# Zero products ahead of the first chunk, a later read of the shared accumulators, and a second gate buffer on one Trainium2 core

## The chip, the cores and the metric

The kernel runs on one core of a Trainium2 chip. The metric is the device time of one launch in microseconds (us), lower is better. All inputs and outputs are float32. The names of the engines are those of the profile: PE is the matrix engine (TensorE; PEld is its weight load), DVE is VectorE, ACT is ScalarE, POOL is GpSimd, and SP (SyncE) issues nearly all of the DMAs.

## What is computed

Three layers in a row: an attention with a pooled and a local part, a bilinear layer, and a layer that multiplies by its own softmax and normalises. The reference, cut to what matters:

```python
B, H, S, D = 4, 8, 576, 64           # attention
q_d, k_d, v_d = (t.reshape(B, H, S // 4, 4, D).mean(axis=3) for t in (q, k, v))
out_d = softmax(scale * q_d @ k_d.T) @ v_d              # 144 pooled positions
mask = np.abs(pos[:, None] - pos[None, :]) < 4
out_local = softmax(np.where(mask, scale * q @ k.T, -1e9)) @ v
x = np.repeat(out_d, 4, axis=2) + out_local             # to 2304 tokens x 512
x = (x @ w_a) * (x @ w_b) @ w_out                       # 512 -> 1536 -> 512
h = x @ w_in                                            # 512 -> 1024
solu = h * softmax(h)
ln = (solu - mean(solu)) / sqrt(var(solu) + 1e-6) * g_ln
out = ln @ w_out2                                       # 1024 -> 512
```

## The kernel before

The 2304 tokens are cut into five blocks: four of 512 tokens (`WIDE`) and a last one of 256. The bilinear layer goes through the 1536 hidden columns in 12 chunks of 128. A chunk of a block is two groups of 12 products into two PSUM tiles called `ab` (`emit_A`, one for `w_a` and one for `w_b`), then a copy of the first to the gate buffer `a` by ACT (`emit_a`), a multiplication by the second on DVE (`emit_mult`), a split of the result into a high part `ph` (ACT) and a low part `pl` (POOL) in `emit_p`, and 12 products into four accumulators (`emit_B`). Every matrix product of these layers is made of three, high by high, high by low and low by high, so the weights are split as well (`w_stages`: `raw` is loaded, then two passes on ACT, two on DVE that write `wm`, a cast on ACT and a subtraction give `w`).

The four accumulators of a wide block are two PSUM tiles `acc0` and `acc1` and the two halves of one tile that spans two banks, `accS`. At the last chunk of a block each is copied out as `o` as soon as its three products are written, and stored to `o1d` in HBM. In the last block two tiles of 512 columns hold all four, each half a tile, and the two `ab` halves of a chunk also share a tile.

Ahead of the first chunk stands the attention of the first 512 tokens. Its pooled part per pair of heads `hp` is: sums of `qkr` to `qkds` (DVE), scores `S` (PE), a maximum `pm` (DVE), exponentials `E` (ACT), a division (POOL), transposes `PT` (PE), a copy `PTs` (ACT), and the product `pv` (PE). Its local part for 128 tokens `s` is: scores `lS` (PE), mask, maximum and subtraction to `lP` (DVE), exponential (ACT), sums `lsm` (DVE), a division (POOL), transposes `lPT` (PE), copies `lPTs` (ACT), the product `lo` (PE), the sum with the pooled part `lx` (DVE), and the split into `xTh` (ACT) and `xTl` (POOL or DVE), which are the operands of the first chunk. `A(0, ...)` of the first chunk is cut in columns 0 to 256, which need `s` = 0 and 1, and 256 to 512, which need 2 and 3.

The order of the work is a list of due times written out by hand (`first` and `add`), played by `advance`. In block 0 the order on every engine is pinned to that list (`pin`), in blocks 1 to 3 that of PE alone, and the rest and the whole last block are ordered by the scheduler's own simulation. An engine takes its instructions strictly in that order.

The third layer (`emit_C` writes `h`, `emit_D` writes `o` from the transposed `cT`) starts in the waits of the last block and then fills the last 170 us.

## Time and profile before

| | |
|---|---|
| runs | 800.87, 805.21, 806.71 us; median 805.21 |
| profiled execution | 803.08 us, of which the span from first to last instruction is 801.3 |
| busy in the span | PE 765.4 us (96%), DVE 376.9 (47%), ACT 332.5 (41%), POOL 228.5 (29%) |
| mean granted TensorE clock | 0.988 of full speed |
| DMA | 85.04 MB, 106 GB/s over the span |

A row of a timeline gives the start, the time that the row covers, the engine, the line of the kernel, the operation with its tiles and shape, and how many instructions were merged. In square brackets stands how long the engine sat idle before and what ended that. [...] A plain float32 product shows as two rows for each instruction, a transpose and the rounded products (`ab`, `acc`, `h`, `o`) as one.

### The profile page before, as it was taken

How to read it: one execution, taken by the hardware profiler on the slowest of the kernel's cores; microseconds unless marked ns; L12 is line 12 of the kernel's file. 1: busy time of each engine (PE TensorE's matmuls, PEld its weight loads, DVE VectorE, ACT ScalarE, POOL GpSimd, SP SyncE). 2: the span in 40 equal slices, each digit the busy share in tenths (PEclk: the TensorE clock that was granted, in tenths of full speed). 3: DMA queues.
4: the chain of work that ended last, by engine and by line, in shares of the span. 5: the costliest groups of instructions: out<-in, count | busy, mean ns of one | idle time of the engine just before them, and what ended most of it. 6: DMA issues, size and time to landing. Idle time of an engine off the chain costs nothing.

```text
span 801.3 us, 12378 instructions
## 1 busy us (share of the span) xinstructions
PE 765.4 (96%) x4848; PEld 621.3 (78%) x4848; DVE 376.9 (47%) x689; ACT 332.5 (41%) x691; POOL 228.5 (29%) x204
## 2 busy tenths in 40 slices
PE   4979999998999999999999999999899999999997
PEld 3867777776787787777787888888788888888885
DVE  5678889974223324223213220126765373545441
ACT  3648777653222324322323221147645343344432
POOL 1242343431322222232111121114222352334320
PEclk9979999999999999999999999999999999999999
DMA  8977844214212203111102000036422554444321
GB/s 239 239 259 246 268 152 137 70 30 139 59 57 61 83 30 110 59 52 34 42 15 80 15 27 1 0 112 208 155 79 66 157 173 144 145 134 145 103 79 40
DMA packets 65226, 85.04 MB, mean 106 GB/s; under 512 B 9016, under 2 KB 46136, under 8 KB 65168
## 3 DMA queue, kind: packets, MB, share of 16 engines
q1 hardware_dynamic: 64864, 84.02, 33.8%
q8 instruction: 38, 0.62, 0.3%
q10 hardware_dynamic: 304, 0.23, 0.1%
q14 instruction: 20, 0.16, 0.1%
HBM read 66.93 MB, written 17.30 MB: 105 GB/s over the span
## 4 chain that ended last, share of the span: by engine, by line
PE 81%; DVE 7%; ACT 5%; DMA 3%; issue 3%; POOL 1%; SPq 0%; DVEq 0%; ACTq 0%; POOLq 0%
PE ab L473 33%; PE o L616 13%; PE h L548 11%; PE acc L507 8%; PE accS L507 7%; PE lo L412 2%; PE pv L283 2%; PE lPT L393 2%; DVE wm L117 2%; DMA qkr<-qkp 1%; PE lS L353 1%; PE S L223 1%; DMA raw<-w 1%; PE PT L266 1%; ACT o L514 1%
## 5 line engine op out<-in xcount | busy, mean ns | idle before, releaser
L473 PE MATMUL ab<-xTh,w 128*128 128x512 f32 (+1 forms) x976 | 298.0, 375 | 6.2 <-DVE a L483 3.6
L473 PEld LDWEIGHTS ab<-xTh,w 128*128 128x128 f32 x976 | 179.9, 191 | 43.7 <-DVE a L483 5.6
L473 PE MATMUL ab<-xTl,w 128*128 128x512 f32 (+1 forms) x488 | 180.2, 369 | 0.9 <-DVE xTl L167 0.5
L490 POOL TENSOR_TENSOR pl<-a,ph 128x512 fp32r<-128x512 f32 (+1 forms) x60 | 75.1, 1251 | 234.6 <-ACT ph L489 234.6
L483 DVE TENSOR_TENSOR a<-a,ab 128x512 f32<-128x512 f32 (+1 forms) x60 | 38.0, 632 | 181.3 <-PE ab L473 181.3
L473 PEld LDWEIGHTS ab<-xTl,w 128*128 128x128 f32 x488 | 93.4, 191 | 15.1 <-DVE xTl L167 0.9
L548 PE MATMUL h<-w,o1w 128*128 128x512 f32 x432 | 103.9, 391 | 1.1 <-ACT w L123 0.9
L548 PEld LDWEIGHTS h<-w,o1w 128*128 128x128 f32 x432 | 80.1, 188 | 18.1 <-ACT w L123 1.1
L616 PE MATMUL o<-w,cTh 128*128 128x512 f32 x288 | 91.0, 397 | 1.2 <-ACT cTh L606 0.9
L507 PE MATMUL acc<-ph,w 128*128 128x512 f32 (+1 forms) x288 | 90.2, 365 | 0.0
L478 ACT COPY a<-ab 128x512 f32<-128x512 f32 (+1 forms) x60 | 32.5, 542 | 108.9 <-PE ab L473 103.7
L507 PE MATMUL accS<-ph,w 128*128 128x512 f32 x192 | 68.0, 391 | 4.2 <-ACT o L514 4.2
L616 PEld LDWEIGHTS o<-w,cTh 128*128 128x128 f32 x288 | 54.0, 188 | 14.3 <-ACT cTh L606 1.1
L489 ACT CAST ph<-a 128x512 fp32r<-128x512 f32 (+1 forms) x60 | 34.6, 577 | 67.2 <-DVE a L483 67.2
L507 PEld LDWEIGHTS acc<-ph,w 128*128 128x128 f32 x288 | 52.2, 189 | 9.1 <-issue 1.2
L616 PE MATMUL o<-w,cTl 128*128 128x512 f32 x144 | 57.2, 397 | 0.1
L507 PE MATMUL acc<-pl,w 128*128 128x512 f32 (+1 forms) x144 | 51.1, 358 | 0.1
L600 POOL TENSOR_TENSOR cTl<-raw,cTh 128x1024 fp32r<-128x1024 f32 x15 | 36.0, 2401 | 44.2 <-ACT cTh L599 36.6
L507 PEld LDWEIGHTS accS<-ph,w 128*128 128x128 f32 x192 | 36.0, 188 | 13.1 <-ACT o L514 5.5
L117 DVE CUSTOM_DVE_ANT_0 wm<-raw,wm 128x1024 uint16<-128x1024 uint16 x52 | 43.4, 845 | 2.3
L255 POOL TENSOR_TENSOR E<-E,ss 72x576 f32<-72x576 f32 x16 | 19.3, 1206 | 81.1 <-DVE ss L253 53.4
L557 DVE TENSOR_REDUCE mx<-h 128x1 f32<-128x1024 f32 x18 | 22.0, 1223 | 43.1 <-PE h L548 43.1
(91 smaller groups left out, 1005.5 us busy)
## 6 DMA issues: line engine op xcount, KB each, us to landing
raw<-w SPq DMA_DIRECT2D x52, 512.0 KB
qkr<-qkp SPq DMA_DIRECT2D x32, 288.0 KB
vd<-v SPq DMA_DIRECT2D x15, 512.0 KB
raw<-vd SPq DMA_DIRECT2D x60, 128.0 KB
vw<-vwin SPq DMA_DIRECT2D x36, 140.0 KB
vp<-vp SPq DMA_DIRECT2D x16, 288.0 KB
o1r<-o1d SPq DMA_DIRECT2D x18, 256.0 KB
out<-ob SPq DMA_DIRECT2D x18, 256.0 KB
```

The costliest lines, as they stand in the source:

```text
L117: DVE.tensor_tensor(out=st["w"], in0=st["w"], in1=st["low"], op=ALU.add)
L255: POOL.tensor_tensor(out=ev, in0=ev, in1=st["ss"].to_broadcast([72, 4, SD]), op=ALU.mult)
L473: PE.matmul(out=abs_[blk, j][n][:, c0:c1], lhsT=w[:, ws], rhs=x[:, k, c0:c1], start=(k == 0 and i == 0), stop=(k == 3 and i == 2), skip_gr ...
L478: ACT.copy(out=a, in_=abs_[blk, j][0])
L483: DVE.tensor_tensor(out=a, in0=a, in1=pb, op=ALU.mult)
L489: ACT.copy(out=ph, in_=a)
L490: POOL.tensor_tensor(out=pl, in0=a, in1=f32(ph), op=ALU.subtract)
L507: PE.matmul(out=accs[blk][m], lhsT=wt[:, ms], rhs=x, start=(j == 0 and i == 0 and (w == WIDE or m % 2 == 0)), stop=(j == NCH - 1 and i == ...
L548: PE.matmul(out=h[:, n * 512:n * 512 + 512], lhsT=x[:, ks], rhs=w, start=(k == 0 and q_ == 0), stop=(k == 3 and q_ == 2))
L557: DVE.tensor_reduce(out=mx, in_=st["h"], axis=AX.X, op=ALU.max)
L600: POOL.tensor_tensor(out=h4(lo), in0=raw, in1=f32(h4(hi)), op=ALU.subtract)
L616: PE.matmul(out=o, lhsT=x[:, k, :], rhs=w, start=(k == 0 and q_ == 0), stop=(k == 7 and q_ == 2))
```

## The change

Three things change. First, products of a tile of zeros, `zz`, are put on PE at ten named places ahead of and in the first chunk: 12 before the first local scores, 9 before those of the second pair of heads, 6 before the fourth, 5 before the first transposes, 7 before the scores `S` of the fourth pair, 6 before the first `lPT`, 10 before the `lo` of `s` = 1, 6 before the second half of `lPT` of `s` = 2, 7 before the columns 256 to 512 of the first chunk, and 4 before the `lS` of `s` = 4. They write to a tile that the following work overwrites, or to one of their own, `fz`. Second, in a wide block the two halves of `accS` are copied out by DVE after the last product of the block, where ACT copied each after its own three products. Third, the gate buffer of the last block is a tile of its own with two buffers, where it was the single buffer of 512 columns.

```diff
+FILL = dict(lS0_0=12, lS0_1=9, lS0_3=6, PT0=5, S3=7, lPT0_0=6, lo1_0=10, lPT2_1=6, A0_256=7, lS4_0=4)
...
+    zz = base.tile([128, 128], F32, name="zz")
+    fz = []
+    def fill(key, out):
+        for _ in range(FILL.get(key, 0)):
+            if out is None:
+                if not fz:
+                    fz.append(ps.tile([128, 512], F32, tag="acc1", name="fz"))
+                out = fz[0][:, 0:128]
+            PE.matmul(out=out, lhsT=zz[:, 0:out.shape[0]], rhs=zz, start=True, stop=True, skip_group_check=True)
...
+            if not b:
+                fill(f"S{hp}", st["S"][0][:, 0:128])
...
+            if not b:
+                fill(f"PT{hp}", st["PT"][0][:, 0:128])
...
+            fill(f"lS{s}_{hps[0]}", None if s > 3 else st["S"][1][:, 384:512])
...
+                fill(f"lPT{s}_{half}", None if s > 1 else pt_[:, 0, :])
...
+                fill(f"lo{s}_{half}", None)
...
+        if (blk, j) == (0, 0):
+            fill(f"A{n}_{c0}", None)
...
     def emit_a(blk, j):
-        a = base.tile([128, WIDE], F32, tag="a", name="a")[:, 0:width[blk]]
+        if width[blk] == WIDE:
+            a = base.tile([128, WIDE], F32, tag="a", name="a")
+        else:
+            a = base.tile([128, 256], F32, tag="a2", bufs=2, name="a")
...
+        def store(m):
+            SP.dma_start(out=o1d[blk][:, :, 128 * m:128 * m + 128].rearrange("i p t -> p i t"),
+                         in_=o1s[blk][:, m, 0:w].rearrange("p (i t) -> p i t", t=128))
...
-                o1 = o1s[blk][:, m, 0:w]
-                ACT.copy(out=o1, in_=accs[blk][m])
-                SP.dma_start(out=o1d[blk][:, :, 128 * m:128 * m + 128].rearrange("i p t -> p i t"),
-                              in_=o1.rearrange("p (i t) -> p i t", t=128))
+                if m < 2 or w < WIDE:
+                    ACT.copy(out=o1s[blk][:, m, 0:w], in_=accs[blk][m])
+                    store(m)
+        if j == NCH - 1 and w == WIDE:
+            for m in (2, 3):
+                DVE.tensor_copy(out=o1s[blk][:, m, 0:w], in_=accs[blk][m])
+                store(m)
...
+    POOL.memset(zz, 0.0)
```

On PE the program began before like this (an entry is a line of the kernel, an operation, its output and inputs, the output's shape and a count of instructions):

```order
L353 MATMUL lS<-qkr 64x70 x4
L223 MATMUL S<-qkds 72x144 x4
L353 MATMUL lS<-qkr 64x70 x4
L223 MATMUL S<-qkds 72x144 x4
L353 MATMUL lS<-qkr 64x70 x8
L223 MATMUL S<-qkds 72x144 x4
L266 MATMUL PT<-id_sb,E 72x72 x8
L223 MATMUL S<-qkds 72x144 x4
L283 MATMUL pv<-PTs,vp 64x144 x16
```

After the change the same stretch on PE reads:

```order
L153 MATMUL lS<-zz 128x128 x12
L372 MATMUL lS<-qkr 64x70 x4
L239 MATMUL S<-qkds 72x144 x4
L153 MATMUL lS<-zz 128x128 x9
L372 MATMUL lS<-qkr 64x70 x4
L239 MATMUL S<-qkds 72x144 x4
L372 MATMUL lS<-qkr 64x70 x4
L153 MATMUL lS<-zz 128x128 x6
L372 MATMUL lS<-qkr 64x70 x4
L239 MATMUL S<-qkds 72x144 x4
L153 MATMUL PT<-zz 72x128 x5
L284 MATMUL PT<-id_sb,E 72x72 x8
```

The real work keeps its order, and the zeros stand between. Further on, PE's order from the transposes of the fourth pair of heads to the `lo` of `s` = 1 is now this, where the entry of `fz` is the only new one:

```order
L284 MATMUL PT<-id_sb,E 72x72 x8
L433 MATMUL lo<-lPTs,vw 64x64 x8
L413 MATMUL lPT<-id_sb,lP 70x128 x8
L433 MATMUL lo<-lPTs,vw 64x64 x8
L301 MATMUL pv<-PTs,vp 64x144 x16
L153 MATMUL fz<-zz 128x128 x10
L433 MATMUL lo<-lPTs,vw 64x64 x16
```

No zeros stand ahead of or behind the transposes `PT` there. On ACT and DVE the order of block 0's start is unchanged.

At the end of block 0 ACT's order was before:

```order
L514 COPY o_2079<-acc_885 128x512
L489 CAST ph<-a 128x512
L514 COPY o_2079<-acc_886 128x512
L514 COPY o_2079<-accS 128x512 x2
L374 ACTIVATE lP<-lP 128x560
```

At the same place DVE's order is after the change:

```order
L509 TENSOR_TENSOR a<-a,ab 128x512
L269 RECIPROCAL ss<-ss 72x4
L549 COPY o_2154<-accS 128x512 x2
L383 TENSOR_TENSOR lP<-lS,mk_sb 128x280 x2
L389 TENSOR_REDUCE lmx<-lP 128x8
```

So two copies have left ACT's queue and stand in DVE's, behind the multiplication of a gate and ahead of a mask.

In the last block PE's order was before, around the first entry of its accumulators (`w_825`, `w_636` and `w_694` are weights of chunks 2, 1 and 0):

```order
L473 MATMUL ab<-xTh,w_825 128x256
L507 MATMUL acc_4938<-ph,w_694 128x256
L507 MATMUL acc_4939<-ph,w_694 128x256
L507 MATMUL acc_4938<-pl,w_694 128x256
L507 MATMUL acc_4938<-ph,w_694 128x256 x2
L507 MATMUL acc_4938<-pl,w_694 128x256
L507 MATMUL acc_4938<-ph,w_694 128x256
L507 MATMUL acc_4939<-pl,w_694 128x256
L507 MATMUL acc_4939<-ph,w_694 128x256 x2
L507 MATMUL acc_4939<-pl,w_694 128x256
L507 MATMUL acc_4939<-ph,w_694 128x256
L473 MATMUL ab<-xTh,w_636 128x256
```

After the change it reads there (`w_900`, `w_1006` and `w_758` are weights of chunks 2, 3 and 0):

```order
L496 MATMUL ab<-xTh,w_900 128x256
L537 MATMUL acc_5013<-ph,w_758 128x256
L537 MATMUL acc_5014<-ph,w_758 128x256
L496 MATMUL ab<-xTh,w_1006 128x256
L496 MATMUL ab<-xTl,w_1006 128x256
L496 MATMUL ab<-xTh,w_1006 128x256 x2
```

The gate products of chunk 3 now begin before the accumulator products of chunk 0 have ended. The rest of the last block is ordered anew on all engines as well. The last 585 instructions of PE are the same in the same order.

## Rows read from the trace of the kernel before

**Rows 1.** The page's first part: busy us, share, instructions.

```profile
PE 765.4 (96%) x4848; PEld 621.3 (78%) x4848; DVE 376.9 (47%) x689; ACT 332.5 (41%) x691; POOL 228.5 (29%) x204
```

**Rows 2.** The waits of PE: total us, times, longest us.

```profile
PE lS L353 <- DMA qkr<-qkp: 9.0, 3, 5.3
PE accS L507 <- ACT o L514: 4.2, 3, 2.5
PE ab L473 <- DVE a L483: 3.6, 3, 2.2
...
PE lo L412 <- DVE lx L424: 2.6, 1, 2.6
```

**Rows 3.** Stretches: busy us of each engine, granted clock, DMA share, GB/s.

```profile
0.00:20.00 20.00, 8.58 (x77) 6.02 (x79) 11.27 (x29) 7.09 (x31) 2.49 (x6) 1.00 0.88 239
...
44.00:45.00 1.00, 1.00 (x19) 0.88 (x18) 0.74 (x1) 0.65 (x2) 1.00 (x1) 0.50 0.98 397
...
193.00:194.00 1.00, 1.00 (x3) 0.73 (x3) 0.93 (x3) 0.00 (x0) 0.00 (x0) 0.50 1.13 335
```

**Rows 4.** Timeline of PE, first 40 us.

```profile
19.38 4.40 PE L283 MATMUL pv<-PTs,vp 72*64 72x144 f32 x32 [1.53 <-ACT PTs L272]
...
32.05 2.18 PE L283 MATMUL pv<-PTs,vp 72*64 72x144 f32 x32
...
35.46 0.45 PE L266 MATMUL PT<-id_sb,E 72*72 72x72 f32 x4 [0.42 <-ACT lPTs L401]
```

**Rows 5.** Timeline of ACT, 33 to 36 us.

```profile
33.17 0.71 ACT L109 ACTIVATE raw<-raw 128x512 f32<-128x512 f32 x1 [0.43 <-DMA raw<-w]
...
34.83 0.58 ACT L401 COPY lPTs<-lPT 70x512 f32<-70x512 f32 x1 [0.37 <-PE lPT L393]
```

**Rows 6.** Timeline of PE, 36 to 56 us.

```profile
36.46 1.07 PE L393 MATMUL lPT<-id_sb,lP 128*70 128x128 f32 x8
...
42.98 1.97 PE L412 MATMUL lo<-lPTs,vw 70*64 70x64 f32 x32 [2.58 <-DVE lx L424]
44.88 2.23 PE L393 MATMUL lPT<-id_sb,lP 128*70 128x128 f32 x8
47.17 1.98 PE L412 MATMUL lo<-lPTs,vw 70*64 70x64 f32 x32
...
54.11 1.15 PE L412 MATMUL lo<-lPTs,vw 70*64 70x64 f32 x32
```

**Rows 7.** The chain that ended last, 47 to 86 us: start, us, what.

```profile
49.15 2.73 PE ab L473 x12
...
52.75 1.43 PE ab L473 x12
...
57.53 1.96 PE ab L473 x11
59.49 1.22 PE S L223 x8
...
84.95 0.65 PE S L223 x8
```

**Rows 8.** The same chain behind the end of block 0, and later.

```profile
192.22 6.95 PE ab L473 x24
...
295.49 5.44 PE ab L473 x24
```

**Rows 9.** Timelines of ACT and DVE, 187 to 191 us.

```profile
187.99 0.68 DVE L483 TENSOR_TENSOR a<-a,ab 128x512 f32<-128x512 f32 x1
...
189.70 0.59 ACT L514 COPY o<-accS 128x512 f32<-128x512 f32 x1
```

**Rows 10.** The chain in the last block, 573 to 576 us.

```profile
573.26 1.75 DVE wm L117
...
575.08 0.34 DVE a L483
```

**Rows 11.** Timeline of PE near the end.

```profile
782.11 1.03 PE L605 MATMUL tp<-id_sb,uw 128*128 128x128 f32 x8
```

## The prediction

> **What bounds the kernel now.** I read the busy shares first. PE is busy for 765.4 of 801.3 us [rows 1], so the kernel is bound by its matrix products. The change takes no product away and adds 72, so it can only gain where PE waits (35.9 us in all) or where it runs at half clock. Next come the waits of PE by cause [rows 2]. The reader is to see four things: 9.0 us are waits for the first loads of `qkr`; 4.2 us, in three waits, are waits for ACT's copies of `accS`; 3.6 us, in three waits, are waits for the gate multiplication in the last block; 2.6 us is one wait of `lo` for `lx`. Third, the clock. In two stretches it stands at 0.50 although PE is busy all the time: around 44 us, behind the `lo` wait, and around 193 us, behind the longest `accS` wait [rows 3]. [...]

> **Zeros ahead of the first chunk: the price.** No row shows a product of zeros. A plain float32 product takes two rows. The nearest row with full weights and 128 columns is `tp`, 8 rows in 1.03 us, 0.13 each [rows 11]: 0.26 us a product, 18.6 for 72. The upper bound is the half clock: `lPT`, 8 rows in 2.23 us [rows 6], 0.28 each, 0.56 a product, 40.3 for all. The lower is `pv`, 2.18 / 32 = 0.07 a row [rows 4], 0.14 a product, 9.8 for all. I take 0.26, since its operands have the same size. Most of it lies in waits: 12 + 9 + 6 products (7.0 us) in the 9.0 us for `qkr` [rows 2], ten (2.6 us) in the 2.6 us for `lx`. What overshoots delays the work behind it, since PE takes its queue in order. The one memset of `zz` falls to POOL, busy for 29% [rows 1], and costs nothing.

> **Zeros: what they can win.** Up to 33 us the clock would save much: the first `pv` alone 4.40 - 2.18 = 2.2 us [rows 4]. But ACT stands in the way. At 33.17 it waited 0.43 us for the load of a weight, `raw`, and behind that in its queue stands the copy `lPTs` at 34.83 [rows 5], for which PE's transposes `PT` wait at 35.46 [rows 4]. The loads of that time do not wait for PE, so `raw` lands no sooner. Of all the gain of the first 33 us, 0.43 us is left. From 42.98 us on the half clock costs what the same work takes at either clock: `lo` 1.97 and 1.98 against 1.15, `lPT` 2.23 against 1.07 [rows 6], 12 products of `ab` 2.73 against 1.43 [rows 7]. On the path are only the second `lo` and `ab`, since ACT and DVE set the time before: 0.83 + 1.30 = 2.13 us. Then 11 products of `ab` in 1.96 against some 1.43 for 12, and `S` 1.22 against 0.65 [rows 7]: 0.53 + 0.57 = 1.10. Together 0.43 + 2.13 + 1.10 = 3.66 us.

> Against this stands a wait that the zeros make. If PE is at least 2.2 us earlier and ACT is not, the wait of `PT` grows from 0.42 us [rows 4] to 2.6 us or more, and no zeros stand there. A wait of 2.58 us is what stood ahead of the half clock at 44 us [rows 6], so I expect half clock from about 35 us on. Then `lo`, `lPT` and `pv` run slow, and the ten zeros ahead of `lo` come after them: `pv` ends 1 to 3 us later than before, the zeros take 2.6 us more, and `lo` of `s` = 1 starts up to 3 us late. Most of that is won back at full clock before the first chunk. I charge 1.66 us, about half of what the stretch wins, and take **2.0 us gained**; the bounds are 3.7 gained (no half clock there) and 1 lost.

> [...] In this trace the clock stayed at half from 42.98 on through `lo` and `lPT`, though PE was busy (1.00 at 44 to 45 us [rows 3]), until after the first `ab`. [...]

> **The read of `accS`.** Before, the second half's products waited for the copy of the first, because both are one tile: 4.2 us in three waits [rows 2]. They go: all 24 products of the block are now written before either copy. The longest also cost the clock: 24 products of `ab` behind it took 6.95 us, against 5.44 at full clock [rows 8], 1.5 us more. Sum 5.7 us. What is late next: two copies stand in DVE's queue, ahead of a mask. ACT's copy took 0.59 us, DVE's read of PSUM of the same size 0.68 [rows 9], so 1.4 us of DVE in all, four times. PE has 24 products of `ab`, 5.4 us [rows 8], in front of it meanwhile, and DVE is busy for 47% [rows 1], so I cost this at nothing; if that cover fails, the price is up to 1.4 us a block. The accumulators are next written two chunks later, and the two stores, a little later in SP's queue, are read in the last block alone. I take **5.5 us**, between 4.2 (waits alone) and 5.7.

> **The second gate buffer.** With one buffer, ACT's copy of a chunk's gate had to wait until `ph` and `pl` of the chunk before were made. Of the three waits of 3.6 us [rows 2] the longest, 2.2, is not of this kind: the multiplication stood behind a `wm` pass of 1.75 us in DVE's queue [rows 10]. The other two, 1.4 us, may go. But the whole last block is ordered anew, on five engines, and its waits cannot be read off an order. I take **1.4 us gained**; the bounds are 5 us gained (all three waits, and 1.4 of the smaller ones) and 3.6 lost (as much waiting again as there was). The tail is untouched: PE's last 585 instructions are the same, and nothing else bounds them.

> **The sum.** 2.0 + 5.5 + 1.4 = 8.9 us. The profiled execution took 803.08, which gives 794.2. The median is 805.21, 2.1 higher, which would give 796.3. I predict the middle, **795.0 us**, 1.3% less.

> **Rivals.** (1) *The start gives nothing.* The half clock holds from the new wait at `PT` until the ten zeros ahead of `lo` have run: ten at 0.56 are 5.6 us in a place where PE used to wait 2.6 us, 3.0 us late, less the 0.43, and the 3.2 us of the later rows only pay this back. For it speaks that the clock was slow to rise at 43 us, against it that `pv`, all products, lies between. Time 794.2 + 2.0 = 796.2 to 798.3, middle 797.3.
> (2) *The last block gets worse.* The new order makes 3.6 us of new waits instead of saving 1.4. For it: products of `ab` for later chunks now go ahead of the accumulators', and the loads of the third layer's weights stand in the same queue. Against it: PE waited little there before, so the work was plentiful. Time 795.0 + 5.0 = 800.0.
> (3) *Slower: the zeros do not lift the clock.* If products of zeros leave the clock at half, all 72 cost 0.56, 40.3 us, in waits that hold 11.4 us in the first 20 (20.00 - 8.58 [rows 3]), 2.6 for `lx` and by my estimate 4 of small ones, 18 in all. Then 22 us stand on the path: 803.1 + 22 - 6.9 = 818. It passes the 1% mark from an overshoot of 17 us on, that is from 0.49 us a product. No row shows zeros, so nothing excludes it; against it speaks that in the rows the clock rose behind any dense products, whatever tile they read, and that real work in between would lift it as before.

> **How the numbers follow.** One per cent, 8.05 us, is about what a measurement of this kernel can tell from no change; the bounds are 797.2 and 813.3. My forecast has 0.55, rival 1 0.20, rival 2 0.15, rival 3 0.05, and 0.05 is left for a better result than forecast, with all bounds at their good end: 3.7 + 5.7 + 5 = 14.4 us, 788.7. Faster by over 1%: most of the forecast (0.45), the better result (0.05), and just under half of rival 1 (0.09), 0.59. Within 1%: the rest of the forecast (0.10), of rival 1 (0.11) and rival 2 (0.15), 0.36. Slower: rival 3, 0.05. The range goes from 789 (the good end) to 802 (rival 2 with 2 us for the spread between runs).

> **What the profile after would show.** Right: no `accS` wait for a copy on PE, and no stretch at 0.50 behind 190 us; the first `pv` in about 2.2 us; `lo` of `s` = 1 in about 1.15 us; a wait of 2.5 us or more of PE at the fourth `PT`, and ACT's third `raw` at about 33 us still waiting for its load; zeros of about 0.13 us a row. `S`, at 59.49 before [rows 7], would start at about 57.5. Wrong: zeros of 0.28 a row with `pv` still at 4.4 (rival 3); half clock from 35 to 45 us (rival 1); more than 4 us of waits for the gate, for weights or for `o1w` between 530 and 630 us (rival 2). A load of `raw` that lands much earlier in another execution would give the start the 2.2 us that I write off.

## The result, and the profile after

The changed kernel took 785.57 us, the median of four executions (782.69 to 790.66); the kernel before, beside it, 803.43 (800.87 to 806.71). The ratio is 0.9745, 95% interval 0.9693 to 0.9797: 2.5% faster, more than the 1.3% forecast and below the range's low end of 789. The profiled execution took 783.45 us, 19.6 less than the profiled one of before. Three executions far off the others of their kernel are left out of the ratios below: 2608.22 us (the kernel before, once more), 806.17 (the zeros alone) and 811.10 (before, beside the last run).

The page's first part, and the waits of PE over the whole span (total us, times, longest us), answer to [rows 1, 2]:

```profile
PE 768.1 (98%) x4992; PEld 629.8 (81%) x4992; DVE 382.5 (49%) x697; ACT 326.7 (42%) x683; POOL 230.6 (30%) x205
```

```profile
PE pv L301 <- ACT PTs L290: 1.6, 3, 1.2
PE lS L153 <- POOL zz L756: 1.0, 1, 1.0
PE PT L284 <- ACT lPTs L421: 0.9, 1, 0.9
PE ab L496 <- ACT a L504: 0.9, 2, 0.5
PE o L650 <- ACT cTh L640: 0.8, 1, 0.8
PE ab L496 <- DVE a L509: 0.8, 1, 0.8
```

PE idles for 13.6 us of 781.7, where it was 35.9 before. The waits for `accS` are gone, the waits for `qkr` are filled with zeros, and of the gate's waits one of 0.8 us is left. The clock, by stretches as in [rows 3], is full in all three:

```profile
0.00:20.00 20.00, 18.73 (x182) 16.60 (x182) 12.01 (x29) 8.00 (x35) 2.69 (x7) 1.00 0.91 255
44.00:45.00 1.00, 1.00 (x14) 0.92 (x11) 1.00 (x2) 0.64 (x2) 0.29 (x1) 1.00 1.01 387
193.00:194.00 1.00, 1.00 (x6) 0.81 (x5) 0.00 (x0) 0.00 (x0) 0.09 (x1) 1.00 0.06 16
```

PE's timeline of the start answers to [rows 4, 6], ACT's to [rows 5]:

```profile
17.77 2.47 PE L301 MATMUL pv<-PTs,vp 72*64 72x144 f32 x32 [0.22 <-ACT PTs L290]
...
31.43 0.44 PE L284 MATMUL PT<-id_sb,E 72*72 72x72 f32 x4 [0.91 <-ACT lPTs L421]
...
36.31 2.50 PE L153 MATMUL fz<-zz 128*128 128x128 f32 x20
38.85 1.15 PE L433 MATMUL lo<-lPTs,vw 70*64 70x64 f32 x32
...
57.71 0.50 PE L496 MATMUL ab<-xTh,w 128*128 128x512 f32 x1 [0.40 <-ACT a L504]
```

```profile
29.67 0.69 ACT L111 ACTIVATE raw<-raw 128x512 f32<-128x512 f32 x1 [1.46 <-DMA raw<-w]
...
30.81 0.57 ACT L421 COPY lPTs<-lPT 70x512 f32<-70x512 f32 x1
```

The first `pv` takes 2.47 us, where it took 4.40 (2.18 at the full clock). The weight that ACT waits for came at 29.67, not at 33.17 [rows 5], so the wait at the fourth `PT` is only 0.91 us, and the clock does not fall behind it (1.00 throughout from 30 to 60 us). The ten zeros ahead of `lo` are 20 rows in 2.50 us, 0.125 a row, 0.25 a product.

To see where the 19.6 us come from, the span is cut at four kinds of rows of PE's timeline: the first 512-column product of `ab` (below also "the chunk", the first one at full width), the last of `accS` in each of the first three blocks, the first 256-column product of the last block, and the last of `o`. The parts, in us:

| kernel | to the first 512-column product | block 0 | block 1 | block 2 | last block to the end |
|---|---|---|---|---|---|
| before | 64.61 | 126.30 | 122.57 | 120.05 | 266.56 |
| after | 57.71 | 123.72 | 119.87 | 119.00 | 260.28 |
| difference | 6.90 | 2.58 | 2.70 | 1.05 | 6.28 |

Block 3 is as long as before (96.2 us). So the start gave 6.9 us (2.0 forecast), the reads of `accS` 2.58 + 2.70 + 1.05 = 6.3 (5.5 forecast), and the last block 6.3 (1.4 forecast). These are the parts of one pair of executions; the start is another in others, as the experiments show.

In two stretches of 60 us each around the last block's products (columns as above), first of before, then of after, PE's idle time falls from 3.92 + 1.67 = 5.59 us to 1.54:

```profile
528.00:588.00 60.00, 56.08 (x357) 49.51 (x356) 35.09 (x65) 37.49 (x72) 19.60 (x17) 1.00 0.51 169
588.00:648.00 60.00, 58.33 (x342) 51.11 (x341) 31.89 (x60) 27.25 (x49) 18.22 (x16) 1.00 0.37 112
```

```profile
515.00:575.00 60.00, 58.46 (x429) 55.31 (x428) 41.17 (x69) 40.19 (x80) 20.54 (x18) 1.00 0.53 172
575.00:635.00 60.00, 60.00 (x297) 50.42 (x296) 29.03 (x60) 25.40 (x44) 20.71 (x17) 1.00 0.40 128
```

Most of the last block's 6.3 us are thus idle time of PE (4.05). Another 1.7 us show as shorter rows: over that block the groups of `ab`, `acc` and `tp` are busy for that much less with the same number of instructions. The last 0.5 us are not traced.

### The profile page after: what moved, and what is told of

It reads as the page before. It is cut to its first block, busy times and chain, and to the rows that moved or that the text cites. A ratio compares the mean times of both kernels' runs of the same rounds, so it can differ in the third digit from the quotient of the medians.

```text
span 781.7 us, 12678 instructions
## 1 busy us (share of the span) xinstructions
PE 768.1 (98%) x4992; PEld 629.8 (81%) x4992; DVE 382.5 (49%) x697; ACT 326.7 (42%) x683; POOL 230.6 (30%) x205
## 5 line engine op out<-in xcount | busy, mean ns | idle before, releaser
L496 PE MATMUL ab<-xTh,w 128*128 128x512 f32 (+1 forms) x976 | 294.5, 372 | 1.9 <-ACT a L504 0.9
L496 PEld LDWEIGHTS ab<-xTh,w 128*128 128x128 f32 x976 | 177.6, 189 | 37.1 <-issue 3.5
```

Of the source, the lines that this page charges most:

```text
L496: PE.matmul(out=abs_[blk, j][n][:, c0:c1], lhsT=w[:, ws], rhs=x[:, k, c0:c1], start=(k == 0 and i == 0), stop=(k == 3 and i == 2), skip_gr ...
```

## The experiments

Three parts were to be told apart, and in the start one question: is the landing of the third weight, on which the forecast of the start rested, the same in every execution? The first four kernels ran side by side on one chip, the next four on another occasion, then three and one. Each group has its own executions of before beside it. "Ratio" is to those, with its 95% interval.

**The kernel before, once more** (no edit).

> The kernel before, unchanged, once more. Theory A (the loads of the start scatter from one execution to the next, whatever the kernel): ACT's third raw starts somewhere between 29.7 and 33.2 us, the first 512-column ab products start at another time than 64.6 (by up to 3.5 us), and the time scatters by the 6 us that its runs already show. Theory B (the zeros themselves bring the loads forward): ACT's third raw starts at 33.2 +- 0.3 again, the first 512-column ab at 64.6 +- 0.5. Time ratio to itself 1.00.

Measured: 805.87 us, ratio 0.999 [0.9947, 1.0032]. In the profiled execution ACT began its third `raw` at 30.35 and the first 512-column product at 62.35, 2.3 us earlier than in the first profile; the rest was as before (last block 266.55). The same instructions therefore reach the chunks at different times, and the forecast's landing at 33.17 was one execution's.

**The zeros alone.**

```diff
+FILL = dict(lS0_0=12, lS0_1=9, lS0_3=6, PT0=5, S3=7, lPT0_0=6, lo1_0=10, lPT2_1=6, A0_256=7, lS4_0=4)
...
+            PE.matmul(out=out, lhsT=zz[:, 0:out.shape[0]], rhs=zz, start=True, stop=True, skip_group_check=True)
...
+    POOL.memset(zz, 0.0)
```

> The zeros alone; all other instructions keep their order on every engine. The prediction's step: 2.0 us faster, first 512-column ab at about 62.6. Theory A: first 512-column ab at 64.6 less 3.7 (what the clock returns) less the scatter of the loads, 57.5 to 61, and 4 to 7 us faster in the time. Theory B: 57.7 as in the changed kernel, 7 us faster, with the third raw on ACT at 29.7.

Measured: 800.86 us, ratio 0.9931 [0.9896, 0.9966]. The profiled execution (802.35) shows the other course of the start, in PE's timeline and ACT's:

```profile
33.71 0.68 PE L284 MATMUL PT<-id_sb,E 72*72 72x72 f32 x4 [2.29 <-ACT lPTs L421]
...
42.13 4.64 PE L153 MATMUL fz<-zz 128*128 128x128 f32 x20
46.69 1.46 PE L433 MATMUL lo<-lPTs,vw 70*64 70x64 f32 x32
...
65.32 0.50 PE L496 MATMUL ab<-xTh,w 128*128 128x512 f32 x1 [0.40 <-ACT a L501]
```

```profile
31.99 0.66 ACT L111 ACTIVATE raw<-raw 128x512 f32<-128x512 f32 x1 [2.87 <-DMA raw<-w]
```

and in stretches:

```profile
30.00:33.00 3.00, 1.42 (x18) 1.05 (x14) 2.80 (x7) 1.01 (x2) 0.00 (x0) 1.00 1.02 390
34.00:38.00 4.00, 4.00 (x42) 3.13 (x42) 1.83 (x3) 3.23 (x7) 0.00 (x0) 0.50 1.24 181
38.00:42.00 4.00, 4.00 (x40) 3.70 (x36) 2.55 (x7) 0.58 (x1) 1.12 (x1) 0.50 0.84 228
42.00:46.00 4.00, 4.00 (x20) 3.88 (x19) 2.83 (x6) 2.50 (x5) 1.53 (x2) 0.50 0.99 387
```

The weight came at 31.99, PE waited 2.29 us for the fourth `PT`, the clock was 0.50 from there to the end of the ten zeros, these took 4.64 us in place of 2.50, and the chunk began at 65.32: no gain, in this execution, over 64.61. That is the course of the first rival. The last block is untouched (266.57). With the other course of the start this execution would take 802.35 - 7.6 = 794.7 us, and one of the twelve, 793.97 at a mean clock of 0.999, is that short. So the median's gain is hardly the clock held up to the chunk.

**The reads of the shared accumulators alone.**

```diff
-                ACT.copy(out=o1, in_=accs[blk][m])
+                if m < 2 or w < WIDE:
+                    ACT.copy(out=o1s[blk][:, m, 0:w], in_=accs[blk][m])
...
+            for m in (2, 3):
+                DVE.tensor_copy(out=o1s[blk][:, m, 0:w], in_=accs[blk][m])
```

> The read of the shared accumulators alone. The prediction's step: no wait of PE for a copy of accS (4.2 us before) and no half clock behind 190 us (1.5), so 5.7 us faster up to the last block. Rival: the 1.5 us of half clock come back elsewhere, 4.2 faster. In the last block the order of the engines changes as well; if that matters more than the buffer, the last block moves by 2 us or more here too.

Measured: 793.1 us, ratio 0.9846 [0.9804, 0.9888]. PE has no wait for `accS`; the first three blocks take 123.70, 119.86 and 119.00 us, 6.4 less than before in sum, the last 264.11, 2.5 less: 8.9 us in all. The profiled execution's other 2.2 us are in the start (62.44), which the edit does not touch and which scatters as seen above. By the medians the gain is 14.7 us, more than the edit's own: all six executions have the mean clock (0.990 to 0.992) that goes with the shorter executions of the kernel before, while most of those beside it are long ones (median 807.79).

**The second gate buffer alone.**

```diff
-        a = base.tile([128, WIDE], F32, tag="a", name="a")[:, 0:width[blk]]
+        if width[blk] == WIDE:
+            a = base.tile([128, WIDE], F32, tag="a", name="a")
+        else:
+            a = base.tile([128, 256], F32, tag="a2", bufs=2, name="a")
```

> The second gate buffer alone. The prediction's step: 1.4 us faster. Theory C (the buffer lets PE run chunks ahead, so that the weights and o1w of the third layer are never late): from the last block's first product to the last o 6 us less than the 266.6 before. Rival D (the saving in the changed kernel came from the order that the scheduler happened to find, with the accS copies on DVE): between 263 and 270 us, either sign.

Measured: 797.53 us, ratio 0.9886 [0.9852, 0.9921]. The last block takes 258.05 us, 8.5 less than before, and PE does not idle at all in the 120 us that answer to those shown of before and after:

```profile
536.00:596.00 60.00, 60.00 (x442) 57.17 (x441) 38.96 (x68) 41.68 (x83) 22.07 (x19) 1.00 0.51 172
596.00:656.00 60.00, 60.00 (x294) 50.19 (x293) 28.86 (x61) 25.88 (x44) 21.42 (x17) 1.00 0.43 132
```

All three waits for the gate multiplication have gone, the one of 2.2 us too. The waits named in the last block add up to 6.2 us before, 0.8 here, 2.4 in the changed kernel. With a single buffer of its own (`bufs=1`; built, not run) the builder writes the order of before on every engine, so the new order comes from the second buffer, and the two were not told apart.

The start of this execution, whose instructions are those of before, is the slowest of all. From PE's timeline:

```profile
34.55 4.11 PE L301 MATMUL pv<-PTs,vp 72*64 72x144 f32 x32
...
54.13 1.98 PE L433 MATMUL lo<-lPTs,vw 70*64 70x64 f32 x32
...
58.52 1.03 PE L413 MATMUL lPT<-id_sb,lP 128*70 128x128 f32 x8
...
71.57 0.50 PE L496 MATMUL ab<-xTh,w 128*128 128x512 f32 x1 [0.40 <-ACT a L504]
```

Here PE stayed at half clock until about 58 us (`pv` 4.11 us at 34.55), where in the first profile it had risen by 32 (2.18). So without zeros the same instructions have two courses: the clock rises before 30 us (eight rows of `PT` took 0.69 us at 29.38 in the first profile, 1.18 at 31.30 here), or not before 58, and the chunk begins at 62 to 65 or at 71.57. The times of the kernel before fit both: in the eleven executions beside the next four kernels seven lie at 798.9 to 801.7 and four at 805.7 to 808.9.

**The changed kernel, once more** (no edit), and three variants beside it.

> The changed kernel, unchanged. Theory A: the start's gain depends on when the load of ACT's third raw lands. If ACT begins that raw by 30 us, the wait ahead of the fourth PT is under 1 us, TensorE's clock stays at 1.00 and the first 512-column product begins near 58 us; if it begins near 32 us, the wait is over 2 us, the clock falls to 0.50 behind it, the ten zeros of fz take over 4 us and the product begins near 65. Medians between 782 and 792. Theory B: the first profile was typical, and every execution begins that product within 1 us of 57.7; medians within 784 to 787.

Measured: 785.08 us (783.41 to 791.36), ratio 0.98 [0.9755, 0.9844]; in the profile the third `raw` began at 30.35, PE waited 0.84 us at the fourth `PT`, and the chunk began at 58.39. The times stand in two groups, each with its own mean granted clock: 783.41 to 785.25 at 0.999 or more, 789.76 and 791.36 at 0.991 (below the lower and the upper group).

**Eight more zeros at the fourth `PT`.**

```diff
-FILL = dict(lS0_0=12, lS0_1=9, lS0_3=6, PT0=5, S3=7, lPT0_0=6, lo1_0=10, lPT2_1=6, A0_256=7, lS4_0=4)
+FILL = dict(lS0_0=12, lS0_1=9, lS0_3=6, PT0=5, S3=7, PT3=8, lPT0_0=6, lo1_0=10, lPT2_1=6, A0_256=7, lS4_0=4)
```

> The changed kernel with eight more products of zeros (2.0 us at the full clock) ahead of the fourth PT. Theory A (the clock that falls behind this wait is what costs, when the load is late): no stretch at 0.50 between 33 and 48 us, the ten zeros of fz near 2.5 us whatever the load does, the 512-column product at 58.5 to 60.5 us; the median from 2 us lower than the changed kernel's to 1 us higher, and its runs closer together. Theory B (the clock there does not follow the wait): the product begins as late as in the changed kernel's own executions or 1 to 2 us later for the added zeros, with a stretch at 0.50 in executions where the load is late.

Measured: 786.78 us (785.43 to 790.43), ratio 0.9819 [0.9777, 0.9862]. The chunk began at 58.56 with no half clock in the profile, but two of five executions still took 790.4. Zeros at this wait alone do not settle it.

**The third and fourth weight load in each other's place.**

```diff
-    for n, f in enumerate([wst[0][0], wst[1][0], locs[0]["loadv"], locs[1]["loadv"], wst[2][0], locs[2]["loadv"],
-                           locs[3]["loadv"]] + [wst[i][0] for i in range(3, 6)]
+    for n, f in enumerate([wst[0][0], wst[1][0], locs[0]["loadv"], locs[1]["loadv"], wst[3][0], locs[2]["loadv"],
+                           locs[3]["loadv"]] + [wst[i][0] for i in (2, 4, 5)]
```

> The changed kernel with the loads of the third and fourth weight tile in each other's place on SP's queue, so that the tile that ACT splits third is fetched some 6 us earlier; every other instruction keeps its place. Theory A (this load's landing makes the wait): ACT's third raw begins at once, by 28.3 us, without a wait for its load; the wait ahead of the fourth PT under 0.6 us; the clock at 1.00 throughout; the 512-column product at 56.5 to 57.7 us; the median 1 to 4 us below the changed kernel's. Theory B (the wait has another end, such as the transposes or DVE): the wait ahead of the fourth PT stays at 0.9 us or more and the time does not change by more than 1 us.

Measured: 784.06 us (781.41 to 789.89), ratio 0.9777 [0.9735, 0.982], 1.0 us below the changed kernel beside it. From the timelines of ACT and of PE:

```profile
27.90 0.70 ACT L111 ACTIVATE raw<-raw 128x512 f32<-128x512 f32 x1
```

```profile
30.73 0.44 PE L284 MATMUL PT<-id_sb,E 72*72 72x72 f32 x4 [0.42 <-ACT lPTs L421]
```

The third `raw` finds its load at once, the wait of PE is half as long, the chunk begins at 57.08, the earliest of all. One of six executions still lies near 790, at a mean clock of 0.991; of the changed kernel's, two of six did.

**The two late reads on ACT in place of DVE.**

```diff
-                DVE.tensor_copy(out=o1s[blk][:, m, 0:w], in_=accs[blk][m])
+                ACT.copy(out=o1s[blk][:, m, 0:w], in_=accs[blk][m])
```

> The changed kernel with the two late reads of accS (the third and fourth of a wide block) on ACT in place of DVE, still after the whole block. Theory A (the place of the reads, not the engine, takes the wait of 4.2 us away): no accS wait in the first four blocks, blocks as short as with the reads on DVE (119.9 and 119.0 us for the second and third block). The last block goes by the order that follows: near 258 us if the copies on DVE are what made it 260.3 beside 258.1 with the gate buffers alone, so 2 us below the changed kernel; Theory B (the engine matters, since ACT reads the gates for the next products too): waits of 0.6 us a block for ACT's a come up at the blocks' borders, and the time is 1 to 3 us above the changed kernel's.

Measured: 787.35 us (783.23 to 789.69), ratio 0.9814 [0.9774, 0.9854]. Blocks 0 to 2 take 123.59, 119.86 and 119.00 us and the last 260.06: with the reads on DVE it was 123.72, 119.87, 119.00 and 260.28. What counts for the blocks is that the reads come after the whole block; the engine does not matter there. The median is 2.3 us above the changed kernel's, as theory B had it, but the profile has none of the waits that B names: two of the six executions lie in the lower group and four at 787.2 to 789.7 with a mean clock of 0.991 to 0.993, so the start's two courses explain it as well. The guess that the copies on DVE cost the last block 2 us was wrong.

**Swapped loads, and three zeros at the fourth `PT`** (`PT3=3` beside the swap above).

> The changed kernel with the third and fourth weight loads in each other's place and three zeros (0.75 us) ahead of the fourth PT, so that neither a late load nor that wait leaves TensorE idle there. Theory A (the clock falls behind this one wait in the slower half of the executions): every execution keeps a mean granted clock of 0.997 or more and lies between 781 and 786 us. Theory B (it falls at another place or by something that no wait of this start sets): a third to a half of the executions still lie near 790 us with a mean clock of 0.990 to 0.994.

Measured: 783.19 us, ratio 0.9734 [0.9687, 0.9781]; all six executions between 782.37 and 785.02, none below a mean clock of 0.999. The changed kernel, run beside it (below), had four of six near 790. Over all its executions (the first four, six and six) the changed kernel has eight at 782.7 to 785.3 with a clock of 0.999 or 1.0, and eight at 787.7 to 792.5 with 0.989 to 0.994; the means are 783.8 and 790.2, 6.3 us apart. With the loads swapped one of twelve is near 790 (this kernel and the one without the zeros at `PT`). So the second group is nearly gone with a weight that lands early. Two things weaken the count: how often each course comes differs between occasions, and the one comparison on a single occasion that is clear, six beside six here, changes the loads and the zeros together.

**The zeros of the first 18 us alone**, in the kernel before.

```diff
-FILL = dict(lS0_0=12, lS0_1=9, lS0_3=6, PT0=5, S3=7, lPT0_0=6, lo1_0=10, lPT2_1=6, A0_256=7, lS4_0=4)
+FILL = dict(lS0_0=12, lS0_1=9, lS0_3=6, PT0=5, S3=7)
```

> The kernel before with the zeros of the first 18 us alone (lS0, PT0, S3), none ahead of the later waits, the accumulators and gate buffers as before. Theory A (the early zeros only make the clock rise by 18 us; without them it rises near 27 us in some executions and near 58 us in others): pv at 18 to 19 us takes 2.5 us in place of 4.4; no execution near 808 us, all between 797 and 803; the clock falls to 0.50 behind the wait for lo, as before, and the first 512-column product begins at 62 to 65 us. Theory B (the later zeros do the work): as the kernel before, with the same two groups near 801 and 808 us.

Measured: 798.9 us, ratio 0.9927 [0.9899, 0.9955]; twelve executions between 795.1 and 800.9; of the seventeen of before beside them six took 805.9 us or more. The first `pv` took 2.47 us at 17.48. The early zeros do one thing: with them the clock rose early, and no execution is as long as the late course makes it. PE's timeline at the next wait:

```profile
26.68 1.07 PE L413 MATMUL lPT<-id_sb,lP 128*70 128x128 f32 x4 [1.58 <-POOL lP L402]
```

Behind it the clock was 0.50 (four rows of `lPT` in 1.07 us, 0.63 at the full clock) until 53.7, and the chunk began at 64.75.

**The changed kernel, a third time.**

> The changed kernel once more. Theory A (two ways through the start, by whether the clock falls between 33 and 48 us): times in two groups near 783.5 and 790 us, the second with a mean clock of 0.990 to 0.994; if the profile falls into the second, it shows a stretch at 0.50 behind a wait of over 2 us ahead of the fourth PT and the ten zeros of fz take over 4 us. Theory B: if the profile falls into the second group, the stretch at 0.50 begins elsewhere.

Measured: 789.61 us (783.55 to 792.52), ratio 0.9795 [0.9744, 0.9847]. The profile fell into the upper group (792.52), and holds a surprise. PE's timeline and ACT's:

```profile
27.43 0.46 PE L301 MATMUL pv<-PTs,vp 72*64 72x144 f32 x2
30.04 3.94 PE L301 MATMUL pv<-PTs,vp 72*64 72x144 f32 x30 [2.15 <-issue]
...
35.65 0.70 PE L284 MATMUL PT<-id_sb,E 72*72 72x72 f32 x4 [0.19 <-ACT lPTs L421]
...
44.08 4.03 PE L153 MATMUL fz<-zz 128*128 128x128 f32 x20
```

```profile
33.10 0.66 ACT L111 ACTIVATE raw<-raw 128x512 f32<-128x512 f32 x1 [4.98 <-DMA raw<-w]
```

Stretches, and the DMA queues from 27.0 to 28.6 us (packets, MB, share of 16 engines):

```profile
25.00:30.00 5.00, 2.84 (x49) 2.15 (x38) 4.79 (x11) 2.64 (x7) 3.31 (x3) 1.00 1.00 229
30.00:34.00 4.00, 3.96 (x31) 3.57 (x32) 1.04 (x3) 0.90 (x2) 0.00 (x0) 0.53 1.04 356
34.00:46.00 12.00, 11.81 (x93) 10.14 (x94) 7.68 (x15) 6.63 (x15) 1.18 (x2) 0.50 0.95 248
```

```profile
q1 hardware_dynamic: 123, 0.31, 94.9%
q8 instruction: 1, 0.02, 5.7%
```

The weight was late again (33.10), but PE stopped before that, for 2.15 us in the midst of `pv`, waiting for nothing that a semaphore shows ("issue"). A packet of 16 KB (38 on this queue are 0.62 MB in the profile of before) on an instruction queue had come through at just that time, among loads that kept the 16 DMA engines busy throughout (DMA share 1.00). In the first profile after such a packet came between 22.7 and 23.8 us, and PE had no gap; in two others with this start it came between 25.3 and 27.05, and PE stopped for 0.5 us at the same place, as in the second profile of the changed kernel:

```profile
28.28 2.17 PE L301 MATMUL pv<-PTs,vp 72*64 72x144 f32 x30 [0.51 <-issue]
```

In four profiles with such a gap PE goes on 1.4 to 1.7 us behind the packet's end: at 28.28 behind 26.6 and at 28.49 behind 27.05 (the two with this start), at 22.24 behind 20.7 (swapped loads and zeros), at 30.04 behind 28.6 here. What makes the gap is not shown; no run moved the packet. With the gap the clock fell to 0.50, from 30 to 47 us, and the chunk began at 66.34. That is theory B's sign: the half clock began elsewhere than at the fourth `PT`, where PE waited 0.19 us. Theory A had the group and the price right.

**The changed kernel without its later zeros** (`FILL` as in the kernel with the first 18 us alone).

> The changed kernel without its 33 later products of zeros (lPT, lo, A0 and lS4; from 25 us on), the 39 early ones kept. Theory A (the early zeros make the clock rise, the later ones fill waits of 1.6 and 2.6 us behind which it would fall): every execution falls to 0.50 from 26 us on, the mean clock is 0.990 or less, and the times make one group near 790 us, 787 to 793, none near 783.5. Theory B (the later zeros are idle weight, and only loads decide): two groups near 783.5 and 790 us, as in the changed kernel.

Measured: 791.38 us (788.32 to 792.35), ratio 0.9833 [0.9783, 0.9882], five of six at a mean clock of 0.980 to 0.985. PE's timeline and the stretches around the first wait that the later zeros would have filled:

```profile
27.83 0.63 PE L413 MATMUL lPT<-id_sb,lP 128*70 128x128 f32 x4 [1.58 <-POOL lP L402]
28.39 1.07 PE L301 MATMUL pv<-PTs,vp 72*64 72x144 f32 x13
30.15 2.54 PE L301 MATMUL pv<-PTs,vp 72*64 72x144 f32 x19 [0.69 <-issue]
```

```profile
25.00:30.00 5.00, 2.88 (x57) 2.30 (x58) 4.83 (x10) 3.12 (x7) 3.30 (x3) 1.00 1.05 298
30.00:35.00 5.00, 4.66 (x33) 3.70 (x32) 3.13 (x7) 2.16 (x4) 0.00 (x0) 0.53 1.01 284
35.00:40.00 5.00, 5.00 (x52) 4.30 (x52) 3.73 (x9) 3.83 (x8) 0.68 (x1) 0.50 0.76 148
```

In this profile a gap of 0.69 us ("issue") follows the wait of 1.58, and the clock fell behind the two together. One execution (788.32 us, clock 0.993) is shorter than theory A allowed, but none reached the lower group. With the later zeros the clock that rose early stayed at 1.00 to 60 us in the changed kernel's first profile; without them it is 0.50 from 35 us here, and with another wait between (the 2.15 us of "issue" above) the zeros did not hold it.

## Why the prediction was wrong

The sign and the parts' places were right: the sum, 2.0 + 5.5 + 1.4, was too small in two of its terms, by 4.9 us each in the profiled pair. Either alone would have left the time near 795.0 - 4.9 = 790.1, inside the range; together they left it.

**The start (2.0 forecast, 6.9 measured): the failed step is "so `raw` lands no sooner. Of all the gain of the first 33 us, 0.43 us is left".** It took the landing of one execution, 33.17, as fixed. In the profiles with zeros and this order of loads ACT began its third `raw` between 29.67 and 33.10. Where it came by 30.35, the wait at the fourth `PT` was 0.4 to 0.9 us, not the 2.6 expected, the clock stayed at 1.00 and the whole gain of the early zeros reached the chunk: the 3.66 us worked out from the half-clock rows and 3 us more. Where it came at 31.99 (the zeros alone), the mechanism of the forecast and of rival 1 followed: a wait of 2.29 us, half clock through `lo`, `lPT`, `pv` and the zeros, and no gain (65.32 beside 64.61). Where it came at 33.10, the clock had fallen before, behind the "issue" gap of 2.15 us (66.34). Both courses were in the text, the half clock as the likely one; the other was a bound (3.7) and a sign of being wrong. The changed kernel lies in either group in half of its executions, 6.3 us apart. The landing is one cause of the upper group, and the swap of two loads suggests that it is the main one; that is not shown, since the changed kernel's one profile of the upper group has the "issue" gap, and with swapped loads and zeros the packet also came early (between 19.5 and 20.7 us, there between 27.0 and 28.6).

The 6.9 us hold luck as well. The second profiles of the two kernels (62.35 and 58.39) give 4.0, and of the 17.9 us between the medians the other two parts leave 17.9 - 6.3 - 6.3 = 5.3 for the start. Nor was the profile of before the right measure of what zeros replace. It had the better of two courses. By the ratio the zeros alone gain 0.69% (0.35 to 1.04), 5.6 us of 807.8: likely because no execution stays at half clock until 58 us any more, which one profile could not show.

Rival 1's point against itself, that `pv`, all products, lies between, did not hold: with the zeros alone the clock stayed at 0.50 behind the last transpose through 4.05 us of `pv` and the 4.64 us of zeros (0.50 from 34 to 46 us, 0.65 from 46 to 48). What brings it back up no run shows.

**The read of `accS` (5.5 forecast, 6.3 measured): right.** (The products of a block's last chunk into the accumulators are 12, not the 24 of the prediction; nothing hangs on it.) No wait, no half clock at 193 us, and the two copies on DVE cost nothing that shows; on ACT they would not either. By itself this part also takes 2.5 us off the last block, through the order that follows.

**The last block (1.4 forecast, 6.3 measured; 8.5 with the gate buffer alone): the failed step is that "the longest, 2.2, is not of this kind".** The multiplication did stand behind a `wm` pass in DVE's queue, but with a second buffer the builder puts `ab` for later chunks and the passes of the weights elsewhere, and that wait goes with the others: with the gate buffer alone all three, 3.6 us, are gone, in the changed kernel all but 0.8. The smaller waits, 2.6 us before, shrink too, and some rows get shorter. The bound of 5 us counted waits alone and was too low. Unlike the start, this part is the same in each profile of the changed kernel (260.2 to 260.3 us). The gains of the parts do not add: 2.5 and 8.5 apart, 6.3 together.

**The price of zeros** (0.26 forecast, 0.25 measured) and rival 3's answer were right: with zeros ahead of it the first `pv` took 2.47 us, without them 4.40. (72 products at 0.26 are 18.7 us, not 18.6, and the middle of 794.2 and 796.3 is 795.25; neither matters.) Rival 2 fell: the new order made no new waits to speak of.

**A better version.** With the two loads swapped and three zeros at the fourth `PT` all executions stay in the lower group: 783.19 us beside 789.61 for the changed kernel on the same occasion. The intervals of the two ratios overlap slightly; what separates them is that none of six, against four of six beside it, is near 790. What the three zeros add to the swap is not shown. Left open: why the clock of the kernel before rises before 30 us in some executions and near 58 in others, and how many of the executions near 790 have a gap of "issue".

## What to carry to other kernels

In this case a landing time and a clock level of the first 60 us were one draw of several (the third `raw`, without the swap, at 29.67 to 33.17 us, the clock up before 30 us or not before 58; the DMA share over these 60 us was 0.93 to 0.94 in the changed kernel): take a second profile, or look whether the times stand in groups and what mean clock each has, before a term is charged to it. Products of zeros cost 0.25 us each here and paid where no wait was left behind which the clock fell; one wait left open (2.29 us behind a late load, 2.15 us of "issue") gave the gain back. When a buffer is added, the whole order of the engines may follow, so the gain is not bounded by the waits that name the buffer.

## What the runs showed of the hardware that was not expected

- The clock fell in or behind waits of PE of 1.58 us (the zeros of the first 18 us alone), 2.15 us ("issue", the changed kernel a third time), 2.29 us (the zeros alone) and 2.58 us (before) in this start; behind 0.91 us (the changed kernel) it did not. It then stayed at 0.50 for 10 to 27 us, with PE busy for most of them. The length of the wait does not decide alone: in the last block of the kernel before the clock stayed at 1.00 behind one of 2.24 us, as PE's timeline and the stretch show:

```profile
575.46 0.39 PE L473 MATMUL ab<-xTh,w 128*128 128x256 f32 x1 [2.24 <-DVE a L483]
```

```profile
575.00:580.00 5.00, 4.54 (x26) 4.01 (x27) 5.00 (x18) 4.06 (x8) 0.87 (x1) 1.00 0.72 256
```
